# Expert slots of a fused attention and two-MoE kernel: gathers three slots ahead, their transposes two, expert reads behind the slot's last transpose

## The chip, the cores and the metric

The kernel runs on one core of a Trainium2 chip. The metric is the device time of one execution in microseconds (us); less is better. A core has five engines with an instruction queue each: TensorE (PE, with PEld for its weight loads), VectorE (DVE), ScalarE (ACT), GpSimd (POOL) and SyncE (SP). Each queue is taken strictly in order. DMAs are issued from a queue (here SP for plain and transposing ones, POOL for indirect ones) and then moved by 16 DMA engines.

## The reference

Three layers follow each other: an attention with exponential features, a gated feed-forward layer, and a mixture of 8 experts in which each token goes to one expert. The change lies in the third:

```python
logits = x @ w_gate + modality_bias[modality_id]
e_idx = np.argmax(logits, axis=1)
...
for e in range(E):
    mask = e_idx == e
    ...
    h = np.maximum(x[mask] @ w1[e], 0.0)
    out[mask] = gate_w[mask, None] * (h @ w2[e])
```

There are 2304 tokens, model width 512, expert width 1024. For the inputs of the reference the experts get 0, 374, 0, 493, 297, 564, 576 and 0 tokens.

## The kernel before

The third layer works in *slots* of 128 tokens of one expert. Every value is held as two half-precision parts, high and low, and a product is three matmuls. A slot `j` takes these steps:

- `gather(j)` (L927): an indirect DMA from POOL's queue fetches the slot's 128 token rows (`xg`, 256 KB) from `xs` in DRAM, by indices that the routing has worked out (`IDX`).
- `xtr(j)` (L933): a transposing DMA on SP's queue makes `xT` of it.
- `wload(j, part)` (L954): SP reads two numbers from SBUF into registers (L956 the expert, L957 whether it differs from the expert that this set of weight tiles already holds), and issues the expert's weights, 2 MB for each part, in two pieces of 1 MB (L963). The pieces are conditional: where the expert is the same, nothing is moved, but the instruction stays in the queue with its waits. There are two sets of weight tiles, L1_0/L2_0 for even slots and L1_1/L2_1 for odd ones; part 0 (L1) waits until `mm1` of slot j-2 has read the set, part 1 (L2) until `mm2` of slot j-2 has.
- `mm1(j)` (L965): 24 matmuls of 512 columns (L973) into two banks; ACT (L976) and DVE (L977) make the two parts of each half of `hs`, and SP transposes each half into `hsT` (L979).
- `mm2(j)` (L982): 24 matmuls (L989), 12 for each half of `hsT`; DVE scales the result (L992), and POOL scatters it to the output (L993).

Slots 0 to 3 are routed from the first 14 of the 18 tiles of tokens, slots 4 and up from all 18, after a second routing step (`hook`) that runs beside the first slots and ends with 18 small matmuls (`inv`, L759). 20 slots always run; three conditional pieces follow, which these inputs do not take.

`run_slots` (L996) writes the steps in the code's order, but what each engine's queue holds is set by a scheduler: the program is built with `schedule_with_timeline_sim=True`, and a model of the times places each instruction as early as the model thinks it can run. `tc.issue_after(x)` keeps what is written under it behind the instruction x. So the order of the queues, printed below, counts, and not the order of the code. The buffers are three `xg`, three `xT` and four `hsT`.

Of the kernel before, what the change touches and what calls it, by code (L numbers as in the profile page):

```python
# [42 lines left out]
M8 = 20  # L43
# [4 lines left out]
def _weave(main, side, lead=0.0):  # L48

    main, side = list(main), list(side)  # L50
    done = 0
    for i, m in enumerate(main):
        m()
        want = min(len(side), int(math.ceil(len(side) * (i + 1) / (len(main) * (1.0 - lead)))))
        while done < want:
            side[done]()
            done += 1
    for s in side[done:]:
        s()
# [3 lines left out]
def body(ctx, tc, k0, kt0, q0, qt0, kk, kkt, qq, qqt, vv, vvt, w_phi, w_gv, w_out, rms_g, mid, w_g2, mbias,  # L63
         w1, w2, consts, out):
    nc = tc.nc
    V, A, G, SP, PE = nc.vector, nc.scalar, nc.gpsimd, nc.sync, nc.tensor
# [855 lines left out]
    IDX, GT, CTL = {}, {}, {}  # L922


    X, HH = {}, {}

    def gather(j):  # L927
        x = (m2 if j >= 2 else xp).tile([128, 2 * DM], F16, tag="xg2", bufs=3 if j >= 2 else 2, name="xg2")
        G.indirect_dma_start(out=x, out_offset=None, in_=xs[0:128 * TA] if j < KA else xs,
                             in_offset=bass.IndirectOffsetOnAxis(ap=IDX[j][0], axis=0))  # L930
        X[j] = x

    def xtr(j):  # L933
        t = (m2 if j >= 2 else xp).tile([128, 8, 128], F16, tag="xT2", bufs=3 if j >= 2 else 2, name="xT2")
        SP.dma_start_transpose(out=t, in_=X[j])
        X[j] = t

    reg = {}

# [11 lines left out]
    def lane_tile(part, lane):  # L951
        return L1[lane].rearrange("p a h l f -> p (a h l f)") if part == 0 else L2[lane].rearrange("p a l f -> p (a l f)")

    def wload(j, part):  # L954
        if part == 0:
            reg[j] = (SP.value_load(CTL[j][0], min_val=0, max_val=NE - 1),  # L956
                      SP.value_load(CTL[j][1], min_val=0, max_val=1))  # L957
        e, need = reg[j]
        src = (ws1, ws2)[part][bass.ds(e, 1)].rearrange("e p f -> (e p) f")
        dst = lane_tile(part, j % 2)  # L960
        for i in range(2):
            sl = slice(4096 * i, 4096 * i + 4096)
            SP.dma_start(out=dst[:, sl], in_=src[:, sl], cond=need, cond_hint=False)  # L963

    def mm1(j, halves=(0, 1)):  # L965
        x, w = X[j], L1[j % 2]
        HH.setdefault(j, [])
        for half in halves:
            p = ps_gv.tile([128, 512], F32, tag="gv", name="m2h") if half == 0 else ps_pj.tile([128, 512], F32, tag="pj", name="m2h")
            n = 0  # L970
            for kc in range(4):
                for xl, wl in PAIRS:
                    PE.matmul(p, lhsT=x[:, 4 * xl + kc, :], rhs=w[:, kc, half, wl, :], start=(n == 0), stop=(n == 11))  # L973
                    n += 1
            hs = m2.tile([128, 2, 512], F16, tag="hs", bufs=4, name="hs")
            A.activation(out=hs[:, 0], in_=p, func=AF.Relu)  # L976
            V.scalar_tensor_tensor(out=hs[:, 1], in0=p, scalar=0.0, in1=hs[:, 0], op0=ALU.max, op1=ALU.subtract)  # L977
            t = m2.tile([128, 8, 128], F16, tag="hsT", bufs=4, name="hsT")
            SP.dma_start_transpose(out=t, in_=hs.rearrange("p a f -> p (a f)"))  # L979
            HH[j].append(t)  # L980

    def mm2(j):  # L982
# [13 lines left out]
    def run_slots(j0, j1, hook=None, started=False):  # L996
        if not started:
            for j in range(j0, min(j0 + 2, j1)):
                gather(j)
                wload(j, 0)  # L1000
                wload(j, 1)
            xtr(j0)
            mm1(j0)
        for j in range(j0, j1):
            if hook is not None:
                hook(j)
            if j + 2 < j1:
                gather(j + 2)
            if j + 1 < j1:
                xtr(j + 1)  # L1010
                mm1(j + 1)
            if j + 2 < j1:
                wload(j + 2, 0)
            mm2(j)
            if j + 2 < j1:
                wload(j + 2, 1)
# [45 lines left out]
    for b in range(4):  # L1062
# [10 lines left out]
        if b == 0:  # L1073
            w = []
            for i, s in enumerate(m0):
                if i % 2 == 0:
# [18 lines left out]
    m7, m8 = group_steps(7, 6), group_steps(8, 7)  # L1095
# [2 lines left out]
    _weave(m7[M7:] + m8[:M8], mixed(w2s[n:], guess(), ra))  # L1098
    wp_ctx.close()
    xp = ctx.enter_context(tc.tile_pool(name="xp", bufs=2, side="right", reuse_waits="tile"))  # L1100
    _weave(m8[M8:], [lambda: gather(0), lambda: gather(1), lambda: xtr(0), lambda: wload(0, 0), lambda: wload(0, 1),
                     lambda: wload(1, 0), lambda: wload(1, 1)])
    for s in out_steps(8):
        s()
# [8 lines left out]
    def hook(j):  # L1113
        while rb and j >= HOOKJ[len(HOOKJ) - len(rb)]:
            used_i[0] = rb.pop(0)()

    mm1(0, (0,))
    for i in range(2):
        with tc.issue_after(last[i]):
            if i == 0:  # L1120
                mm1(0, (1,))
            else:
                run_slots(0, NSURE, hook, True)
    used = nc.values_load(used_i[0], min_val=0, max_val=NSLOT)  # L1124
    for j0, j1 in ((20, 21), (21, 23), (23, 25)):
        with tc.If(used > j0):
            run_slots(j0, j1)
# [72 lines left out]
```

## Time and profile before

| | us |
|---|---|
| median of 3 runs | 941.72 (937.82 to 948.75) |
| the profiled execution | 947.29 |
| its span, first to last instruction | 945.5 |
| TensorE busy in the span | 831.9 (88%) |
| VectorE busy | 525.8 (56%) |
| SP queue's transfers, share of 16 DMA engines | 76.1% |

The durations below come from the profiled execution, which took 1.8 us more than its span. The slots fill the last 240 us of the span. "SPq" rows are DMA issues on SP: the time from the first issue of a run of like ones to the end of the last, not the transfer. An `L` in a row is a weight tile, `m2h` the result of `mm1`, `m2y` that of `mm2`.

### The profile page before, as it was taken

How to read it: one execution, taken by the hardware profiler on the slowest of the kernel's cores; microseconds unless marked ns; L12 is line 12 of the kernel's file. 1: busy time of each engine (PE TensorE's matmuls, PEld its weight loads, DVE VectorE, ACT ScalarE, POOL GpSimd, SP SyncE). 2: the span in 40 equal slices, each digit the busy share in tenths (PEclk: the TensorE clock that was granted, in tenths of full speed). 3: DMA queues.
4: the chain of work that ended last, by engine and by line, in shares of the span. 5: the costliest groups of instructions: out<-in, count | busy, mean ns of one | idle time of the engine just before them, and what ended most of it. 6: DMA issues, size and time to landing. Idle time of an engine off the chain costs nothing. (4 is left out here: it accounts for less than half of the span.)

```text
span 945.5 us, 18474 instructions
## 1 busy us (share of the span) xinstructions
PE 831.9 (88%) x6760; PEld 569.7 (60%) x6760; DVE 525.8 (56%) x1160; ACT 423.9 (45%) x1093; POOL 383.4 (41%) x384
## 2 busy tenths in 40 slices
PE   8944989978978988788998899998999787999995
PEld 7833778557567657476766578675764333444442
DVE  7788788877556755568767744347726211222221
ACT  5666446556466866776557734334321010111110
POOL 1567645347255945547745535121220212121001
PEclk9755989999999999999999989999999988999998
DMA  8778778599888989898979853997995389799631
GB/s 297 198 189 186 178 168 214 171 227 236 211 209 248 273 253 237 235 238 224 238 216 224 203 115 57 330 333 250 284 320 105 101 214 191 145 287 241 168 87 51
DMA packets 266591, 197.40 MB, mean 209 GB/s; under 512 B 212863, under 2 KB 214271, under 8 KB 262912
## 3 DMA queue, kind: packets, MB, share of 16 engines
q1 hardware_dynamic: 263296, 186.21, 76.1%
q0 software_dynamic: 3200, 9.97, 3.2%
q8 instruction: 55, 0.90, 0.4%
q14 instruction: 40, 0.33, 0.1%
HBM read 164.92 MB, written 43.52 MB: 220 GB/s over the span
## 5 line engine op out<-in xcount | busy, mean ns | idle before, releaser
L515 PE MATMUL gv<-xT,wgv 128*128 128x256 f16 x2304 | 285.7, 281 | 25.4 <-DVE hu L525 18.4
L515 PEld LDWEIGHTS <-wgv 128*128 128x128 f16 x2592 | 254.6, 100 | 70.8 <-issue 26.3
L152 POOL TENSOR_TENSOR hT<-hu,hT 128x256 f16<-128x256 f32 x108 | 84.8, 785 | 197.1 <-ACT hT L151 191.7
L631 DVE SCALAR_TENSOR_TENSOR w2b<-w2a,w2b 128x512 f16<-128x512 f32 x128 | 107.1, 837 | 94.2 <-ACT w2b L630 93.5
L537 PE MATMUL po<-wo,hT 128*128 128x512 f16 x648 | 155.0, 388 | 0.5 <-POOL wo L152 0.3
L630 ACT ACTIVATE w2b<-w2a 128x512 f16<-128x512 f32 x128 | 81.2, 635 | 109.2 <-DMA w2a<-in_w_dram 101.9
L989 PE MATMUL m2y<-L,hsT 128*128 128x512 f16 x480 | 109.8, 385 | 8.2 <-DMA hsT<-hs 8.2
L152 POOL TENSOR_TENSOR eq<-e,eq 128x512 f16<-128x512 f32 x72 | 90.3, 1260 | 63.9 <-DVE eq L149 28.4
L973 PE MATMUL m2h<-L,xT 128*128 128x512 f16 x480 | 109.7, 385 | 5.5 <-DMA xT<-xg 5.3
L976 ACT ACTIVATE hs<-m2h 128x512 f16<-128x512 f32 x40 | 23.9, 597 | 193.4 <-PE m2h L973 181.5
L537 PEld LDWEIGHTS <-hT 128*128 128x128 f16 x648 | 62.8, 100 | 68.7 <-issue 7.6
L989 PEld LDWEIGHTS <-hsT 128*128 128x128 f16 x480 | 47.3, 99 | 66.4 <-DMA hsT<-hs 9.2
L973 PEld LDWEIGHTS <-xT 128*128 128x128 f16 x480 | 47.4, 99 | 64.1 <-DMA xT<-xg 5.8
L977 DVE SCALAR_TENSOR_TENSOR hs<-m2h,hs 128x512 f16<-128x512 f32 x40 | 27.6, 691 | 99.7 <-ACT hs L976 99.1
L523 DVE SCALAR_TENSOR_TENSOR th<-th,gv 128x256 f32<-128x256 f32 x108 | 44.6, 413 | 53.2 <-ACT th L522 52.7
L993 POOL DMA_INDIRECT out_dram<-y,ixB x16 | 16.0, 997 | 127.1 <-DVE y L992 110.6
L151 ACT CAST hT<-hu 128x256 f16<-128x256 f32 x108 | 43.7, 405 | 46.8 <-DVE hu L525 46.4
L360 ACT ACTIVATE e<-pj,b 128x128 f32<-128x128 f32 x144 | 54.0, 375 | 9.7 <-POOL eq L152 8.1
L387 PE MATMUL oo<-kv,eT 128*128 128x65 f16 x768 | 33.7, 204 | 27.0 <-DMA eT<-eq 25.5
L522 ACT ACTIVATE th<-gv 128x256 f32<-128x256 f32 x108 | 41.5, 384 | 34.9 <-PE gv L515 34.6
L361 ACT ACTIVATE e<-pj,b 128x128 f32<-128x128 f32 x144 | 54.7, 380 | 0.2 <-DVE b L354 0.2
L320 PE MATMUL kv<-v,ek 128*128 128x65 f32 (+1 forms) x320 | 49.5, 300 | 2.7 <-ACT ek L296 2.6
(229 smaller groups left out, 1157.7 us busy)
## 6 DMA issues: line engine op xcount, KB each, us to landing
L<-ws SPq DMA_DIRECT2D x88, 1024.0 KB
w2a<-in_w_dram SPq DMA_DIRECT2D x128, 256.0 KB
ws<-w2b SPq DMA_DIRECT2D x128, 256.0 KB
wst<-in_w_gv_dram SPq DMA_DIRECT2D x24, 512.0 KB
wst<-in_w_out_dram SPq DMA_DIRECT2D x12, 512.0 KB
xs<-x SPq DMA_DIRECT2D x18, 256.0 KB
v<-in_vv_dram SPq DMA_DIRECT2D x16, 260.0 KB
k<-in_kk_dram SPq DMA_DIRECT2D x12, 256.0 KB
```

The source lines that it names most:

```text
L151: A.copy(dst_hi, src)
L152: (V if lo == "v" else G).tensor_tensor(out=dst_lo, in0=src, in1=dst_hi, op=ALU.subtract)
L320: PE.matmul(acc[:, s, :], lhsT=l, rhs=r_, start=(n == 0), stop=(n == len(ops) - 1))
L360: A.activation(out=e[:, r, 0, :], in_=pp[:, j, :], func=AF.Exp, scale=sc, bias=b1[:, j:j + 1])
L361: A.activation(out=e[:, r, 1, :], in_=pp[:, j, :], func=AF.Exp, scale=-sc, bias=b2[:, j:j + 1])
L515: PE.matmul(p[:, which, :], lhsT=w[:, kc, wl, f], rhs=x[:, 4 * xl + kc, :], start=(n == 0), stop=(n == 11))
L523: V.scalar_tensor_tensor(out=t, in0=t, scalar=1.0, in1=p[:, 0, :], op0=ALU.add, op1=ALU.mult)
L537: PE.matmul(p, lhsT=hT[g, c][:, hl, tk], rhs=wo[:, c, wl, :], start=(c == 0 and hl == 0 and wl == 0), stop=(c == 11 and hl == 1))
L630: A.activation(out=o[:, :, 0, :], in_=t, func=AF.Copy, scale=WS)
L631: V.scalar_tensor_tensor(out=o[:, :, 1, :], in0=t, scalar=WS, in1=o[:, :, 0, :], op0=ALU.mult, op1=ALU.subtract)
L973: PE.matmul(p, lhsT=x[:, 4 * xl + kc, :], rhs=w[:, kc, half, wl, :], start=(n == 0), stop=(n == 11))
L989: PE.matmul(p, lhsT=t[:, 4 * hl + i, :], rhs=w[:, fc, wl, :], start=(fc == 0 and hl == 0 and wl == 0), stop=(fc == 7 and hl == 1))
```

## The change

The gather of a slot is written three slots ahead in place of two, its transpose two slots ahead in place of one, and `wload` of part 0 (the two register reads and the L1 pieces) of slot j+2 is kept behind the last `hsT` transpose of slot j.

```diff
     def xtr(j):
         t = (m2 if j >= 2 else xp).tile([128, 8, 128], F16, tag="xT2", bufs=3 if j >= 2 else 2, name="xT2")
-        SP.dma_start_transpose(out=t, in_=X[j])
         X[j] = t
+        SP.dma_start_transpose(out=t, in_=G2.pop(j))
...
-            SP.dma_start_transpose(out=t, in_=hs.rearrange("p a f -> p (a f)"))
+            LAST[j] = SP.dma_start_transpose(out=t, in_=hs.rearrange("p a f -> p (a f)")).ins
...
             xtr(j0)
             mm1(j0)
+            if j0 + 1 < j1:
+                xtr(j0 + 1)
+        else:
+            gather(j0 + 2)
         for j in range(j0, j1):
             if hook is not None:
                 hook(j)
+            if j + 3 < j1:
+                gather(j + 3)
             if j + 2 < j1:
-                gather(j + 2)
+                xtr(j + 2)
             if j + 1 < j1:
-                xtr(j + 1)
                 mm1(j + 1)
             if j + 2 < j1:
-                wload(j + 2, 0)
+                with tc.issue_after(LAST.pop(j)):
+                    wload(j + 2, 0)
             mm2(j)
...
-    _weave(m8[M8:], [lambda: gather(0), lambda: gather(1), lambda: xtr(0), lambda: wload(0, 0), lambda: wload(0, 1),
+    _weave(m8[M8:], [lambda: gather(0), lambda: gather(1), lambda: xtr(0), lambda: xtr(1), lambda: wload(0, 0), lambda: wload(0, 1),
```

How the scheduled queues differ, at the three places that matter below. First SP's queue from the `hsT` transposes of slot 3 to the token transpose of slot 4 (`xT_10719` before, `xT_10631` after), before the change:

```order
L979 DMA_TRANSPOSE hsT<-hs 128x8x128 x2
L956 TENSOR_LOAD ctlB
L956 ISA x2
L963 ISA
L963 DMA L_0_8739<-ws_74 128x4096
...
L963 DMA L_1_8738<-ws_73 128x4096
L957 TENSOR_LOAD ctlB
L957 ISA x2
...
L935 DMA_TRANSPOSE xT_10719<-xg_10625 128x8x128
```

The second "..." stands for eight more such reads, L956 and L957 in turn; nine others stand right ahead of the first row. After the change:

```order
L979 DMA_TRANSPOSE hsT<-hs 128x8x128 x2
L963 ISA
L963 DMA L_0_8739<-ws_74 128x4096
L956 TENSOR_LOAD ctlB
L956 ISA x2
L957 TENSOR_LOAD ctlB
L957 ISA x2
L963 ISA
L963 DMA L_0_8739<-ws_74 128x4096
...
L963 DMA L_1_8738<-ws_73 128x4096
L936 DMA_TRANSPOSE xT_10631<-xg_10537 128x8x128
```

Nine reads between became two, and both pieces of slot 4's second weights (`L_0_8739`) stand behind the `hsT` transposes, the two reads between them.

Second, TensorE's queue where `mm1` of slot 5 ends, before the change (`xT_10811` is slot 5, `xT_10903` slot 6):

```order
L973 LDWEIGHTS xT_10811
L973 MATMUL m2h<-L_1_8738,xT_10811 128x512
L973 LDWEIGHTS xT_10903
L973 MATMUL m2h<-L_0_8737,xT_10903 128x512
L973 LDWEIGHTS xT_10903
```

After the change (`xT_10723` is slot 5; `L_0_8739` with `hsT` is `mm2` of slot 4):

```order
L973 LDWEIGHTS xT_10723
L973 MATMUL m2h<-L_1_8738,xT_10723 128x512
L989 LDWEIGHTS hsT
L989 MATMUL m2y<-L_0_8739,hsT 128x512
L989 LDWEIGHTS hsT
```

Before, `mm1` of slot 6 begins right behind `mm1` of slot 5; after, all of `mm2` of slot 4 and half of `mm2` of slot 5 (36 matmuls) stand ahead of it, and `mm1` of slot 7 ahead of `mm2` of slot 6.

Third, SP's queue around the first weights of slot 6 (`L_0_8737`) and the first piece of its second weights (`L_0_8739`), before the change; the four `hsT` rows are the halves of slots 4 and 5, `xT_10995` is slot 7, `xT_11087` slot 8:

```order
L963 DMA L_0_8737<-ws_73 128x4096
L979 DMA_TRANSPOSE hsT<-hs 128x8x128
L963 ISA
L963 DMA L_0_8737<-ws_73 128x4096
L979 DMA_TRANSPOSE hsT<-hs 128x8x128
L935 DMA_TRANSPOSE xT_10995<-xg_10901 128x8x128
L979 DMA_TRANSPOSE hsT<-hs 128x8x128
L935 DMA_TRANSPOSE xT_11087<-xg_10993 128x8x128
L979 DMA_TRANSPOSE hsT<-hs 128x8x128
L963 ISA
L963 DMA L_0_8739<-ws_74 128x4096
```

After the change, where both `hsT` rows are slot 5:

```order
L979 DMA_TRANSPOSE hsT<-hs 128x8x128
L957 TENSOR_LOAD ctlB
L957 ISA x2
L963 ISA
L963 DMA L_0_8737<-ws_73 128x4096
L963 ISA
L963 DMA L_0_8737<-ws_73 128x4096
L979 DMA_TRANSPOSE hsT<-hs 128x8x128
L963 ISA
L963 DMA L_0_8739<-ws_74 128x4096
```

The first weights (`L_0_8737`) moved behind the first `hsT` transpose of slot 5, both pieces together, and the first piece of the second weights (`L_0_8739`) now follows one transpose later in place of five.

## Rows read from the trace of the kernel before

**Rows 1.** TensorE's timeline, slots 2 to 19: start us, us, engine line operation.

```profile
735.40 2.75 PE L989 MATMUL m2y<-L,hsT 128*128 128x512 f16 x12
...
743.17 2.75 PE L989 MATMUL m2y<-L,hsT 128*128 128x512 f16 x12
748.49 5.35 PE L989 MATMUL m2y<-L,hsT 128*128 128x512 f16 x24 [2.56 <-DMA hsT<-hs]
759.15 15.64 PE L973 MATMUL m2h<-L,xT 128*128 128x512 f16 x60 [5.30 <-DMA xT<-xg]
774.63 2.75 PE L989 MATMUL m2y<-L,hsT 128*128 128x512 f16 x12
777.58 1.89 PE L973 MATMUL m2h<-L,xT 128*128 128x512 f16 x8 [0.20 <-DMA L<-ws]
...
782.76 5.34 PE L989 MATMUL m2y<-L,hsT 128*128 128x512 f16 x24
793.72 5.07 PE L989 MATMUL m2y<-L,hsT 128*128 128x512 f16 x12 [5.62 <-DMA hsT<-hs]
798.62 5.34 PE L973 MATMUL m2h<-L,xT 128*128 128x512 f16 x24
...
853.01 5.34 PE L989 MATMUL m2y<-L,hsT 128*128 128x512 f16 x24
...
925.53 10.52 PE L989 MATMUL m2y<-L,hsT 128*128 128x512 f16 x48
```

**Rows 2.** Busy time by stretch: us, PE PEld DVE ACT POOL, granted PE clock, DMA, GB/s.

```profile
759.15:765.00 5.85, 5.85 (x16) 2.20 (x17) 0.00 (x0) 0.53 (x1) 1.95 (x2) 0.56 0.67 148
...
793.70:798.60 4.90, 4.88 (x12) 1.76 (x13) 0.00 (x0) 0.00 (x0) 0.67 (x1) 0.52 0.98 283
798.60:935.70 137.10, 137.10 (x637) 62.15 (x635) 27.73 (x39) 15.52 (x26) 21.20 (x22) 1.00 0.68 169
```

**Rows 3.** SP's timeline of DMA issues, 735 to 797 us.

```profile
735.74 3.58 SPq L963 DMA_DIRECT2D L<-ws  x4
745.23 2.62 SPq L979 DMA_TRANSPOSE hsT<-hs  x2
749.79 0.83 SPq L963 DMA_DIRECT2D L<-ws  x3
755.86 6.73 SPq L935 DMA_TRANSPOSE xT<-xg  x3
...
767.90 0.34 SPq L963 DMA_DIRECT2D L<-ws  x1
...
782.44 0.33 SPq L963 DMA_DIRECT2D L<-ws  x1
782.87 1.30 SPq L979 DMA_TRANSPOSE hsT<-hs  x1
...
789.57 7.09 SPq L979 DMA_TRANSPOSE hsT<-hs  x1
```

**Rows 4.** The tile hs on DVE, 741 to 747 us: min/median/max ns, first and last start.

```profile
L977 DVE SCALAR_TENSOR_TENSOR hs<-m2h,hs x2: 691/692/692, 742.7 to 744.0; 128x512 f16<-128x512 f32 x2
```

**Rows 5.** Register reads on SP by line, 750.5 to 756 us.

```profile
L956 SPq TENSOR_LOAD <-ctlB x4: 262/267/273, 751.3 to 754.7; - x4
...
L957 SPq TENSOR_LOAD <-ctlB x5: 262/270/272, 750.7 to 755.2; - x5
```

**Rows 6.** POOL's timeline, the first gather of the second routing step (slot 4).

```profile
736.55 0.98 POOL L929 DMA_INDIRECT xg<-xs,ixB  x1 [3.75 <-DVE iBg L768]
```

**Rows 7.** DMA queues (packets, MB, share) and issues by line, 700 to 946 us.

```profile
q1 hardware_dynamic: 67520, 29.50, 55.4%
...
L<-ws SPq DMA_DIRECT2D x72, 1024.0 KB
```

**Rows 8.** SP's timeline of DMA issues around slot 11.

```profile
826.45 2.21 SPq L963 DMA_DIRECT2D L<-ws  x4
...
838.47 1.78 SPq L963 DMA_DIRECT2D L<-ws  x4
...
844.24 5.76 SPq L979 DMA_TRANSPOSE hsT<-hs  x2
```

More of the change, by code (lines that the diff above doesn't have):

```diff
@@ L922, in body @@
     IDX, GT, CTL = {}, {}, {}
-    X, HH = {}, {}
+    X, G2, HH, LAST = {}, {}, {}, {}
     def gather(j):
@@ L930, in gather @@
                              in_offset=bass.IndirectOffsetOnAxis(ap=IDX[j][0], axis=0))
-        X[j] = x
+        G2[j] = x
     def xtr(j):
         t = (m2 if j >= 2 else xp).tile([128, 8, 128], F16, tag="xT2", bufs=3 if j >= 2 else 2, name="xT2")
-        SP.dma_start_transpose(out=t, in_=X[j])
         X[j] = t
+        SP.dma_start_transpose(out=t, in_=G2.pop(j))
     reg = {}
```

## The prediction

> **What bounds the kernel now.** I read the clock and the share of TensorE over the span first, then TensorE's timeline over the last stage (the 20 slots of the second mixture of experts), then the DMA issues of SP beside it. In the timeline [rows 1] a slot is two blocks: 24 matmuls of `mm1` (L973) and 24 of `mm2` (L989). From 798.62 to 925.53 us stand 588 matmuls, 126.91 us, so 215.8 ns each, 5.18 us a block and 10.36 us a slot; TensorE is busy for all 137.10 us of that stretch at full clock [rows 2]. There nothing can be gained by ordering. Before it the timeline has holes. After the routing matmuls (from 735.40 us) 840 matmuls are left; at 215.8 ns they take 181.3 us and would end at 916.7 us. They end at 925.53 + 10.52 = 936.05 us, of which 0.16 us is the drawn-out end of the last one. So 19.2 us are lost, all between 745 and 799 us:
>
> - before `mm2` of slot 3: 748.49 - (743.17 + 2.59) = 2.7 us, for the transpose of `hs`
> - before `mm1` of slot 4: 759.15 - (748.49 + 5.18) = 5.5 us, for the transpose of the gathered tokens
> - 60 matmuls from 759.15 to 774.63: 15.48 us where 12.95 are due, 2.5 us
> - before the second half of `mm1` of slot 6: 0.4 us, for its weights
> - before the first half of `mm2` of slot 6: 793.72 - (782.76 + 5.18) = 5.8 us
> - 12 matmuls from there: 4.90 us where 2.59 are due, 2.3 us.
>
> The third and sixth are the clock: 0.56 and 0.52 of full speed, which is the 1.2 GHz level, right behind the two long holes [rows 2]. The hole of 2.7 us left no such mark: the blocks behind it run at 5.18 us.
>
> Who makes the holes? On SP [rows 3] the issues are in one line. After four weight issues end at 735.74 + 3.58 = 739.32 us, the next one, the `hs` transposes of slot 3, starts at 745.23 us, though the first `hs` was ready at 742.7 + 0.7 = 743.4 us [rows 4]. The order on SP has nine register reads in between (of expert numbers for slots far ahead). The same again: the weight issues from 749.79 end at 750.62 us, the transpose of slot 4 starts at 755.86 us, and between them stand nine reads; five of L957 and four of L956 lie in 750.5 to 756 us, 0.26 to 0.27 us of load each [rows 5], and with the register work behind each load 5.24 / 9 = 0.58 us a read. The gather of slot 4 was not to blame: its indices were there at 736.55 us [rows 6].
>
> The hole at slot 6 is another one. Few weight loads really run: 72 pieces of 1 MB are issued from 700 us on, but the SP queue moved 29.5 MB there [rows 7], of which some 61 transposes and two stores take 0.26 MB each, 16.5 MB. That leaves 13 MB, three slots of 4 MB. Counting tokens per expert in the reference's inputs (0, 374, 0, 493, 297, 564, 576, 0) puts them at slots 6, 11 and 14. Slot 6 is the bad one: TensorE takes it right behind slots 4 and 5, so its first weights wait for the late `mm1` of slot 4, its second weights for the late `mm2` of slot 4 (issued from 782.44 us), and the `hs` transposes queue behind them (782.87, then one that holds SP for 7.09 us) [rows 3].
>
> **The change, part by part.** Gathers: three ahead in the code; but the POOL queue has them in the same places as before up to slot 9, so nothing, either way (a gather that came 1 us later would cost 0 where TensorE has 10 us of cover, and at most that 1 us at slot 4). Transposes two ahead: in the full stretch the scheduler already had a slot's token transpose ahead of the `hs` transposes of the slot three earlier, and `mm1` never waits there [rows 2], so nothing there. Issuing a slot's reads and first weights behind the last `hs` transpose: this spreads the reads, two a slot. No read is added; four A-phase reads move from before 690 us to slots 0 and 1. TensorE has no hole there (its first is at slot 3), so I take 0 for it, between a loss and a gain of 0.5 us.
>
> I walk TensorE's new order with 2.59 us a half block and 5.18 us a block. The 120 slot matmuls ahead of the routing matmuls are the same set, so 735.40 us stands. `mm1` of slot 3 to 740.6, `mm2` of 2 to 745.8, `mm2` of 3 to 750.9, `mm1` of 4.
>
> - *`hs` of slot 3.* Before, its second half was ready at 744.0 + 0.7 us [rows 4], 1.5 us after the block ended at 743.17 [rows 1]; now 742.1 us. From issue to first use took 748.49 - 745.23 = 3.3 us, so even that half is there at 745.4; needed are the first half at 745.8 and the second at 748.4. Hole gone: 2.7 gained.
> - *Tokens of slot 4.* SP now has them behind the second half of slot 4's second weights, which must wait for `mm2` of slot 2 (745.8), and two more weight issues; three issues took 0.83 us, so 746.7 us; issue to use took 759.15 - 755.86 = 3.3, so 750.0 against 750.9. Only 0.9 us to spare: I take a hole of 0.3 us, 0 to 2. Gain 5.5 and the 2.5 of clock, less 0.3.
> - *First weights of slot 6.* They now follow the first `hs` transpose of slot 5. `mm1` of 4 to 756.1, of 5 to 761.3, its first half to 758.7; + 1.5 + 1.3 (a transpose on SP) + 0.6 (a read): 762.1 us, the second piece 762.6. Before, that piece was issued at 767.90 and TensorE had it at 777.58, 9.7 us later: now 772.3. Needed: `mm2` of 4 (to 766.4) and half of `mm2` of 5 (to 769.0) now stand in front, then 12 matmuls, 771.6. Hole 0.7 us, 0 to 3.
> - *Second weights and `hs` of slot 6.* `mm1` of 6 ends at 774.9, then half of 5 (777.5) and `mm1` of 7 (782.7). The first `hs` transpose goes out about 776.2. Before, issue to use was 793.72 - 782.87 = 10.9 us, which would give 787.1, a hole of 4.4. At slot 11 the first weights went out by 828.7 (four issues from 826.45), the second from 838.47, the `hs` transposes from 844.24, and `mm2` started at 853.01 without a wait [rows 8, 1]: 24.3 us from first weights to use were enough, 8.8 us from transpose to use too. Slot 6 now has 762.6 to 782.7, 20.1 us. Bounds 0 and 4.4; I take 2, in the middle.
>
> The Trainium skill (DMA: Bandwidth & Descriptors, Queues, rings and completion order) says that each DMA engine takes the descriptors of one issuing queue in ring order. Rows 3 agree: a transpose behind weights was ready 10.9 us after issue, one without 3.3 us. By that rule alone all that is ahead must have moved first, and with all 4 MB ahead of the transpose the hole would be the upper 4.4 us, the gain 13.8. The new order issues the first half of the second weights some 12 us ahead of the transpose, which is why the sum does not go by that.
>
> What waits behind the new waits: the second weights' second half waits for a whole `mm2` on SP, and behind it stand the next slot's first weights and a token transpose; at slot 4 that is the 0.9 us above, and in the full stretch the transposed tokens are for a slot more than 20 us off.
>
> Sum: 19.2 - 0.3 - 0.7 - 2 = 16.2 us. From the profiled execution's 947.29 us: 931.1. The median of the runs shown is 941.72, 5.6 us lower; the holes are a matter of queue order, not of that difference, so I take the same off it: 925.5 us. In the full stretch SP now also reads registers in every slot: 3 transposes of 1.3, four weight issues of up to 2.2 together, 2 reads of 0.6, 7.3 us of 10.36. Hidden; if not, it is the second rival.
>
> **Rivals.**
> 1. *The weights of slot 6 keep their hole.* For: the load's 4 MB has 4 us less than it had at slot 11. Then 3 + 4.4 us of holes, 2.3 of clock behind them, and 2 at slot 4: gain 19.2 - 11.7 = 7.5, 934 us. Against: slots 11 and 14 show no wait at all.
> 2. *SP becomes the bound: slower.* In the slots with loads SP is held by full queues (5.76 us for two transposes at 844.24 [rows 8], 7.09 for one [rows 3]). If reads and held transposes bring its slot over 10.36 us, tokens come late in every slot from 7 to 19. A slot of 12.5 us costs 2.1 x 12 = 25 us against 16 gained: 951 us. Against: a held queue means that engines are moving data, and only three slots load.
> 3. *The change does not do what it says.* The scheduler had the token transposes early already; if the holes belong to the routing (indices at 736.55) they only move. No change, 941.7. Against: 1.2 to 5.2 us of reads stand in the very gaps.
>
> **How the numbers follow.** Forecast 0.70, first rival 0.17, second 0.06, third 0.07. A measurement here tells about 1% (9.4 us) from nothing. The forecast has all but little of its chance over that, and of the first rival about half: faster 0.77. Same: the rest of these two and the third, 0.17. Slower: the second, 0.06. Range: all bounds at their best give 925.5 - 3 - 0.5, so 922, less a microsecond of spread of the runs: 921; at their worst (2, 3, 4.4, clock 2.3, 0.5) 935, and 2 us more for the spread and the edge of the third rival: 937.
>
> **What would show it.** In TensorE's timeline after: no hole at slots 3 and 4, `mm1` of slot 4 near 751; two reads between weight issues on SP in each slot; clock 1.00 from 735 on; a hole of 0 to 4 us before `mm2` of slot 6; the last matmul near 920. Wrong, if TensorE still stands over 5 us before slot 4 or slot 6, or if holes appear past slot 7.

## The result, and the profile after

The changed kernel takes 936.26 us (median of 20 runs, 929.64 to 940.44), the kernel before 944.75 us (20 runs, 936.02 to 948.75). The ratio is 0.9916, with a 95% interval of 0.9894 to 0.9938: 0.84% of 944.75 us are 7.9 us, between 5.9 and 10.0. The time lies in the range of the forecast (921 to 937 us), near its upper end. The gain is just under half of the 16.2 us that it had worked out, and under the 1% that it had called the least that can be told; with 20 runs of each the interval leaves out 1 all the same.

The page of the changed kernel: busy time, and the granted TensorE clock in 40 slices of 23.4 us. The profiled execution took 939.29 us, its span 937.5.

```profile
PE 825.2 (88%) x6760; PEld 568.7 (61%) x6760; DVE 524.6 (56%) x1160; ACT 424.3 (45%) x1093; POOL 380.9 (41%) x384
...
PEclk9755897999999999999899999999999999999998
```

The busy share of TensorE is the one of before, 88%: holes went, and with them 831.9 - 825.2 = 6.7 us of its busy time, most of which had been half clock (2.5 and 2.3 us in the prediction's list). The timeline shows both. TensorE after, in the same form as [rows 1]; slot 0 starts at 711.07 us, the last `mm2` ends at 917.55 + 10.52 = 928.07 us:

```profile
711.07 2.75 PE L973 MATMUL m2h<-L,xT 128*128 128x512 f16 x12
...
739.49 5.34 PE L973 MATMUL m2h<-L,xT 128*128 128x512 f16 x24
744.66 10.52 PE L989 MATMUL m2y<-L,hsT 128*128 128x512 f16 x48
755.43 10.53 PE L973 MATMUL m2h<-L,xT 128*128 128x512 f16 x48 [0.24 <-DMA xT<-xg]
765.80 7.93 PE L989 MATMUL m2y<-L,hsT 128*128 128x512 f16 x36
774.38 2.75 PE L973 MATMUL m2h<-L,xT 128*128 128x512 f16 x12 [0.65 <-DMA L<-ws]
777.93 2.75 PE L973 MATMUL m2h<-L,xT 128*128 128x512 f16 x12 [0.80 <-DMA L<-ws]
782.39 2.76 PE L989 MATMUL m2y<-L,hsT 128*128 128x512 f16 x12 [1.71 <-DMA hsT<-hs]
784.99 5.34 PE L973 MATMUL m2h<-L,xT 128*128 128x512 f16 x24
791.59 5.35 PE L989 MATMUL m2y<-L,hsT 128*128 128x512 f16 x24 [1.25 <-DMA hsT<-hs]
...
853.76 5.34 PE L989 MATMUL m2y<-L,hsT 128*128 128x512 f16 x24
859.35 5.35 PE L973 MATMUL m2h<-L,xT 128*128 128x512 f16 x24 [0.25 <-DMA L<-ws]
865.74 5.35 PE L989 MATMUL m2y<-L,hsT 128*128 128x512 f16 x24 [1.03 <-DMA hsT<-hs]
...
917.55 10.52 PE L989 MATMUL m2y<-L,hsT 128*128 128x512 f16 x48
```

The blocks of slots 2 to 5 now follow each other: the holes of 2.7 and 5.5 us of before are one of 0.4. At slot 6 there are four short holes in place of a short and a long one, and at slot 14 (859.35 and 865.74) there are two that before did not have. Busy time by stretch after, as in [rows 2]:

```profile
774.38:796.78 22.40, 18.64 (x85) 8.06 (x86) 3.52 (x5) 2.39 (x4) 2.98 (x3) 1.00 1.02 240
796.78:859.35 62.57, 62.32 (x289) 28.09 (x288) 13.02 (x19) 7.16 (x12) 11.97 (x12) 1.00 0.81 211
859.35:870.93 11.58, 10.54 (x49) 4.64 (x49) 1.92 (x3) 1.19 (x2) 1.99 (x2) 1.00 1.13 286
```

The clock is 1.00 in every one, where before had 0.56 and 0.52 [rows 2]. And SP's DMA issues after, as in [rows 3]:

```profile
748.85 2.74 SPq L963 DMA_DIRECT2D L<-ws  x4
751.69 4.32 SPq L936 DMA_TRANSPOSE xT<-xg  x3
...
762.50 4.39 SPq L979 DMA_TRANSPOSE hsT<-hs  x2
768.32 1.04 SPq L963 DMA_DIRECT2D L<-ws  x2
769.47 2.84 SPq L979 DMA_TRANSPOSE hsT<-hs  x1
...
778.52 4.35 SPq L963 DMA_DIRECT2D L<-ws  x4
782.98 1.97 SPq L936 DMA_TRANSPOSE xT<-xg  x1
785.05 4.55 SPq L979 DMA_TRANSPOSE hsT<-hs  x2
```

The gap of 5 us between weight issues and the next transpose, in which SP read registers, is gone (748.85 + 2.74 = 751.59, then 751.69). The first weights of slot 6 go out at 768.32 us, and a transpose right behind them at 769.47.

**How the profiles add up.** I call *stage* the time from the first matmul of slot 0 to the end of the last `mm2`, *ahead* what comes before it; about 11 us of tail follow. Ahead of the stage the kernels differ only in where a few reads and one token transpose stand on SP.

| profile | ahead, us | stage, us | ratio to before, 95% |
|---|---|---|---|
| before, three profiles | 707.0, 714.0, 707.4 | 229.0, 226.1, 227.0 | 1 |
| changed, two profiles | 711.1, 711.7 | 217.0, 218.4 | 0.9916 [0.9894, 0.9938] |
| reads_only | 710.3 | 217.7 | 0.9911 [0.9872, 0.9950] |
| ahead_only | 709.4 | 227.6 | 1.0017 [0.9984, 1.0049] |
| reads_early | 707.0 | 220.8 | 0.9962 [0.9934, 0.9990] |
| before_no_loads | 706.3 | 219.2 | 0.9947 [0.9914, 0.9981] |
| after_no_loads | 710.3 | 210.4 | 0.9839 [0.9799, 0.9879] |
| after_half_loads | 706.9 | 213.3 | 0.9861 [0.9803, 0.9918] |
| weights_early | 706.5 | 218.1 | 0.9914 [0.9885, 0.9943] |
| weights_on_act | 712.0 | 259.2 | 1.0262 [1.0161, 1.0364] |
| weights_early_act | 710.1 | 233.8 | 0.9997 [0.9950, 1.0043] |

The profiles of weights_on_act and weights_early_act are of slow runs of these kernels (982.41 and 956.37 us), while the ratios count the fast ones alone (959.18 and 973.40 us, and 935.90 to 945.24), so in these two rows stage and ratio do not belong together.

With no hole and full clock the stage would be 229.0 - 19.2 = 209.8 us. The time ahead scatters by 7.7 us between two kernels with the order of before (706.3 and 714.0), so two single profiles do not give the gain; the stage does better. On the mean it fell from 227.4 to 217.7, by 9.7 us, which lies within the interval of the ratio.

### The profile page after: what moved, and what is told of

It reads as the page before. It is cut to its first block, busy times and chain, and to the rows that moved or that the text cites. A ratio compares the mean times of both kernels' runs of the same rounds, so it can differ in the third digit from the quotient of the medians.

```text
span 937.5 us, 18475 instructions
## 1 busy us (share of the span) xinstructions
PE 825.2 (88%) x6760; PEld 568.7 (61%) x6760; DVE 524.6 (56%) x1160; ACT 424.3 (45%) x1093; POOL 380.9 (41%) x384
## 5 line engine op out<-in xcount | busy, mean ns | idle before, releaser
L515 PE MATMUL gv<-xT,wgv 128*128 128x256 f16 x2304 | 282.7, 279 | 26.5 <-DVE hu L525 19.4
L537 PE MATMUL po<-wo,hT 128*128 128x512 f16 x648 | 151.5, 382 | 1.9 <-DVE x L545 1.9
L989 PE MATMUL m2y<-L,hsT 128*128 128x512 f16 x480 | 106.7, 379 | 4.0 <-DMA hsT<-hs 4.0
L973 PE MATMUL m2h<-L,xT 128*128 128x512 f16 x480 | 107.0, 379 | 1.9 <-DMA L<-ws 1.7
L976 ACT ACTIVATE hs<-m2h 128x512 f16<-128x512 f32 x40 | 23.9, 597 | 181.4 <-PE m2h L973 181.4
L387 PEld LDWEIGHTS <-eT 128*128 128x128 f16 x768 | 30.9, 105 | 40.1 <-DMA eT<-eq 39.0
```

The costliest lines, as they stand in the source:

```text
L387: PE.matmul(acc[:, j, :], lhsT=et[:, hl * 8 + j * 2 + s, :], rhs=kvs[2 * p + j % 2][:, vl, s, :], start=(n == 0), stop=(n == 5))
L515: PE.matmul(p[:, which, :], lhsT=w[:, kc, wl, f], rhs=x[:, 4 * xl + kc, :], start=(n == 0), stop=(n == 11))
L537: PE.matmul(p, lhsT=hT[g, c][:, hl, tk], rhs=wo[:, c, wl, :], start=(c == 0 and hl == 0 and wl == 0), stop=(c == 11 and hl == 1))
L989: PE.matmul(p, lhsT=t[:, 4 * hl + i, :], rhs=w[:, fc, wl, :], start=(fc == 0 and hl == 0 and wl == 0), stop=(fc == 7 and hl == 1))
```

## The experiments

**The two kernels once more.** Unchanged copies. In the first pair of profiles the stage of the changed kernel was 12.0 us shorter, the whole time only 8: 4.06 us more lay ahead of the stage. One theory was that the change costs something there, the other that this scatters.

> The changed kernel once more, for a second profile. Slot stage is the time from the first mm1 matmul of slot 0 to the end of the last mm2 matmul: 229.0 us before, 217.0 us after in the first two profiles; the part ahead of it was 707.0 us before and 711.1 after. Theory A (the 4.1 us ahead of the stage are scatter between executions): stage 216 to 219 us again, part ahead anywhere in 704 to 712. Theory B (the change itself makes the part ahead longer): part ahead 710 to 712 again. Ratio by both 0.990 to 0.994.

> The kernel before once more, for a second profile. The changed kernel's stage came out at 217.0 and 218.4 us, 11 us under the 229.0 us of before, but its time only 8 us under. Theory C (the first profile of before shows a stage longer than is usual for it, and a part ahead of the stage shorter than usual): stage 223 to 227 us, part ahead 708 to 712 us. Theory D (the stage is what it was, and the change lengthens the part ahead): stage 228 to 230 us, part ahead 706 to 708.

> The kernel before, a third profile. The stage was 229.0 and 226.1 us, and 227.6 us in the kernel with gathers and transposes ahead alone, the part ahead of it between 706.3 and 714.0 us in ten profiles whatever the kernel. Expected: stage 226 to 229 us, part ahead 706 to 714 us.

The second runs of the changed kernel gave 0.9913 [0.9881, 0.9944] and 939.63 us against 946.51, the time ahead 711.65 us. Before's second profile had 714.0 us ahead, its third 707.4. The changed kernel's 711.65 us had fitted both theories; before's 714.0 lies above what either had expected of it, and two kernels with the order of the change have 706.9 and 706.5 (after_half_loads, weights_early). So the 4.06 us are scatter; that the change costs a microsecond or two there is not excluded.

**One half of the change at a time.** Only the rule of order on the reads and first weights, put into the kernel before:

```diff
-            SP.dma_start_transpose(out=t, in_=hs.rearrange("p a f -> p (a f)"))
+            LAST[j] = SP.dma_start_transpose(out=t, in_=hs.rearrange("p a f -> p (a f)")).ins
...
-                wload(j + 2, 0)
+                with tc.issue_after(LAST.pop(j)):
+                    wload(j + 2, 0)
```

> The kernel before with one part of the change: the register reads and first weights of slot j+2 behind the last hsT transpose of slot j; gathers and token transposes written as before. The scheduled queues of TensorE and SP come out as in the changed kernel but for a few rows. Theory A (the register reads made the holes): stage 216 to 220 us, ratio 0.989 to 0.994, as the whole change. Rival (the gathers and transposes written ahead bring the gain): stage 227 to 231 us, ratio 0.998 to 1.002.

And the changed kernel without that rule, so only gathers and transposes further ahead:

```diff
-                with tc.issue_after(LAST.pop(j)):
-                    wload(j + 2, 0)
+                wload(j + 2, 0)
```

> The changed kernel without the rule that keeps reads and first weights behind the last hsT transpose: gathers three and transposes two slots ahead alone. SP again has nine reads ahead of the hsT transposes of slot 3 and nine ahead of the token transpose of slot 4, TensorE's order is that of before. Theory A: stage 227 to 231 us with both long holes and half clock behind them, ratio 0.998 to 1.002. Rival: stage 216 to 220 us, ratio 0.989 to 0.994.

The rule alone gives 0.9911 [0.9872, 0.9950], all of the gain. Gathers and transposes alone give 1.0017 [0.9984, 1.0049], nothing. TensorE's timeline of ahead_only has the holes of before, at their places:

```profile
750.41 5.35 PE L989 MATMUL m2y<-L,hsT 128*128 128x512 f16 x24 [2.08 <-DMA hsT<-hs]
761.05 15.29 PE L973 MATMUL m2h<-L,xT 128*128 128x512 f16 x60 [5.28 <-DMA xT<-xg]
...
794.45 5.29 PE L989 MATMUL m2y<-L,hsT 128*128 128x512 f16 x12 [4.88 <-DMA hsT<-hs]
```

In that of reads_only the wait for slot 4's tokens is 0.28 us, and slot 6 keeps a wait:

```profile
754.67 10.53 PE L973 MATMUL m2h<-L,xT 128*128 128x512 f16 x48 [0.28 <-DMA xT<-xg]
...
790.62 5.35 PE L989 MATMUL m2y<-L,hsT 128*128 128x512 f16 x24 [3.01 <-DMA hsT<-hs]
```

So it is not the tokens that had come late by their own gathers or by the place of their transposes; SP came late to them.

**The reads spread, but the weights free.** The rule moves the reads and the first weights, and with them TensorE's order (`mm1` of slot 6 behind `mm2` of slot 4). Here only the reads are bound, one slot earlier than their weights, and the scheduler goes back to before's order on TensorE:

```diff
-    def wload(j, part):
-        if part == 0:
+    def wread(j):
+        if j not in reg:
             reg[j] = (SP.value_load(CTL[j][0], min_val=0, max_val=NE - 1),
                       SP.value_load(CTL[j][1], min_val=0, max_val=1))
+
+    def wload(j, part):
+        wread(j)
...
-                with tc.issue_after(LAST.pop(j)):
-                    wload(j + 2, 0)
+                wload(j + 2, 0)
             mm2(j)
             if j + 2 < j1:
                 wload(j + 2, 1)
+            if j + 3 < j1 and (j + 3 < KA or j >= 1):
+                with tc.issue_after(LAST[j]):
+                    wread(j + 3)
```

> The changed kernel, with the two reads of a slot split from its first weights: the reads stand behind the last hsT transpose of the slot three ahead, the first weights are free again. TensorE's order is that of before (mm1 of slot 6 right behind slot 5, mm2 of slot 6 right behind slot 5), but SP has one or two reads where before had nine. Theory A1 (the reads alone made the long holes, TensorE's order does not matter): no hole over 1 us ahead of slot 4, stage 216 to 221 us, ratio 0.989 to 0.995. Theory A2 (half of the gain is TensorE's order, which gives the load of slot 6 more time): hole ahead of slot 4 gone, but 5 us or more of holes at slot 6, perhaps with half clock behind them; stage 220 to 226 us, ratio 0.994 to 0.998.

It gives 0.9962 [0.9934, 0.9990], so 3.6 us, under half of the gain; by the stage it is 227.4 - 220.8 = 6.6 us of 9.7, two thirds. TensorE's timeline (lines are three further down, L976 is `mm1`, L992 `mm2`):

```profile
752.50 10.53 PE L976 MATMUL m2h<-L,xT 128*128 128x512 f16 x48 [0.51 <-DMA xT<-xg]
...
765.43 2.75 PE L976 MATMUL m2h<-L,xT 128*128 128x512 f16 x12 [2.40 <-DMA L<-ws]
...
785.71 4.06 PE L992 MATMUL m2y<-L,hsT 128*128 128x512 f16 x12 [4.59 <-DMA hsT<-hs]
```

The wait before slot 4 is gone here too, so the spread reads do that by themselves. At slot 6 stand 2.40 and 4.59 us, the second with half clock behind it (a granted clock of 0.66, and 3.90 us to the next block where 2.59 are due): 8.6 us lost, as before had (0.4 + 5.8 + 2.3). So the second theory of the expectation came true. What TensorE's new order and the later place of the first weights are worth together, most of it at slot 6, is about 220.8 - 217.7 = 3.1 us of stage, or 0.9962 - 0.9911 = 0.51%, 4.8 us, by the ratios; one profile does not decide between the two.

**Without the loads.** To part the reads from the weights, the flag that says whether a slot's expert differs was made zero, in the kernel before and in the changed one; all instructions stay in their queues, and the weight loads of slots 4 to 19 (slots 6, 11 and 14 in fact) move nothing:

```diff
-            V.tensor_tensor(out=ctl[:, 1, 0:2], in0=e[:, 0:2], in1=S["eidA"][:, KA - 2:], op=ALU.not_equal)
-            V.tensor_tensor(out=ctl[:, 1, 2:], in0=e[:, 2:], in1=e[:, 0:NB - 2], op=ALU.not_equal)
+            V.tensor_tensor(out=ctl[:, 1, 0:2], in0=e[:, 0:2], in1=e[:, 0:2], op=ALU.not_equal)
+            V.tensor_tensor(out=ctl[:, 1, 2:], in0=e[:, 2:], in1=e[:, 2:], op=ALU.not_equal)
```

> The kernel before with the weight loads of slots 4 to 19 left out: the register that says whether a load is needed is always 0 there, so slots 6, 11 and 14 and those after them use the wrong expert's weights. Reads, waits and issue order stay. Theory (in the kernel before the two long waits ahead of slot 4 come of the reads, the one at slot 6 of its load): holes of 2.7 and 5.5 us and the half clock behind them stay, those at slot 6 go, stage 219 to 222 us. Rival (the loads hold SP or the DMA engines and so make the holes ahead of slot 4 too): stage 209 to 213 us.

> The changed kernel with the weight loads of slots 4 to 19 left out in the same way. Theory (what holes are left in the changed kernel, 6.7 us at slots 5 to 7 and 13 to 14, come of the loads of slots 6 and 14): stage 210 to 212 us. Rival (they come of the reads that now stand in every slot, or of the order of the transposes): stage 215 to 218 us.

The changed kernel's stage falls to 210.4 us, 0.6 above the one without holes. Before's stays at 219.2. Its TensorE timeline, without loads:

```profile
747.29 7.04 PE L989 MATMUL m2y<-L,hsT 128*128 128x512 f16 x24 [2.09 <-DMA hsT<-hs]
757.87 14.81 PE L973 MATMUL m2h<-L,xT 128*128 128x512 f16 x60 [3.53 <-DMA xT<-xg]
...
780.28 7.93 PE L989 MATMUL m2y<-L,hsT 128*128 128x512 f16 x36
```

The holes of slots 3 and 4 are there with no load running, those of slot 6 are not: two troubles, as the prediction had it. Now each part of the gain has its own number, from one profile of each kernel without loads. Reads: 219.2 - 210.4 = 8.8 us of stage, and by the ratios 0.9947 - 0.9839 = 1.08%, 10.2 us. Loads: they cost 227.4 - 219.2 = 8.2 us of stage before and 217.7 - 210.4 = 7.3 after, so 0.9 us were gained; by the ratios they cost 0.53% before and 0.77% after, so nothing was. The intervals are some 3 us wide to either side, and both ways of reading put the loads' part near nothing.

**Half the bytes.** If the holes at slots 6 and 14 are waits for weights to move, they should shrink with the bytes; if they are waits in SP's order, they should stay. Each piece from slot 4 on loads half of its columns, the other half is left out:

```diff
-            sl = slice(4096 * i, 4096 * i + 4096)
+            sl = slice(4096 * i, 4096 * i + (4096 if j < 4 else 2048))
```

> The changed kernel in which each weight piece of slots 4 to 19 moves only the first half of its columns, so slots 6, 11 and 14 load 2 MB in place of 4 and multiply by weights that are partly those of another expert. The stage was 217.0, 218.4 (changed) and 210.4 us (no loads). If the holes that the change left are the time that the bytes take on the DMA engines: half or less of the 7.3 us stays, stage 211 to 214 us. If any load costs that much by its place among the transposes, whatever its size: 216 to 218 us.

The stage is 213.3 us: 210.4 with none, 217.7 with all, so of the loss of 7.3 us by the loads 2.9 are left with half the bytes. The holes at slot 14 are gone, at slot 6 the first weights and the `hs` of slot 5 still wait, on TensorE:

```profile
771.89 3.83 PE L973 MATMUL m2h<-L,xT 128*128 128x512 f16 x17 [0.88 <-DMA L<-ws]
...
777.63 2.76 PE L989 MATMUL m2y<-L,hsT 128*128 128x512 f16 x12 [1.69 <-DMA hsT<-hs]
```

So the loss goes with the bytes in the main, as the first theory had it, but not everywhere: the wait for the `hs` of slot 5 is 1.69 us with half of them and was 1.71 with all. The ratio's interval, 0.9803 to 0.9918, does not part this kernel from the changed one, and its queue on SP came out a little differently (three weight issues, not two, stand ahead of that transpose), so this rests on one profile.

**First weights written a slot earlier.** If the late issue at 768.32 us is what costs at slot 6, first weights that stand earlier on SP should cure it. They stay behind the same transposes, but come ahead of the second weights of the slot before:

```diff
+        if j0 + 2 < j1:
+            with tc.issue_after(LAST.pop(j0)):
+                wload(j0 + 2, 0)
         for j in range(j0, j1):
...
-            if j + 2 < j1:
-                with tc.issue_after(LAST.pop(j)):
-                    wload(j + 2, 0)
+            if j + 3 < j1:
+                with tc.issue_after(LAST.pop(j + 1)):
+                    wload(j + 3, 0)
```

> The changed kernel with reads and first weights of slot j+3 behind the last hsT transpose of slot j+1, in place of slot j+2 behind slot j: on SP the first weights of a slot now come ahead of the second weights of the slot before it, and do not wait for that mm2. If the holes at slots 6 and 14 come of weights issued too late: stage 212 to 215 us, no wait for weights (L), ratio 0.984 to 0.989. If they come of the 4 MB that must move in any case: stage 216 to 219 us, the waits at other places, ratio 0.990 to 0.994.

0.9914 [0.9885, 0.9943], no better than the changed kernel. TensorE still waits for the first weights of slot 6, here 0.99 us for the first piece, and at slot 14 for `hs`, with half clock behind it (24 matmuls in 7.00 us, granted clock 0.76):

```profile
767.92 2.75 PE L973 MATMUL m2h<-L,xT 128*128 128x512 f16 x12 [0.99 <-DMA L<-ws]
...
870.95 7.00 PE L989 MATMUL m2y<-L,hsT 128*128 128x512 f16 x24 [2.21 <-DMA hsT<-hs]
```

This does not settle the question, because the weights won no time against their use. They went out at 762.58 us at the earliest, and TensorE, which has only `mm2` of slot 4 ahead of `mm1` of slot 6 in this kernel, was due there at 767.92 - 1.15 = 766.77, 4.2 us later; in the changed kernel it is 765.80 + 3 x 2.59 - 768.32 = 5.3 us. Whether an earlier issue would close the holes of slot 6 was not tried.

**Weights from another queue.** If the transposes are late because weights stand ahead of them in SP's queue, weights issued from ACT's queue should free them. The reads and loads of slots 2 to 19 go to ACT, in the changed kernel and in weights_early; `LAST[j]` is then the activation that makes `hs`:

```diff
     def wload(j, part):
+        Q = A if 2 <= j < NSURE else SP
...
-            reg[j] = (SP.value_load(CTL[j][0], min_val=0, max_val=NE - 1),
-                      SP.value_load(CTL[j][1], min_val=0, max_val=1))
+            reg[j] = (Q.value_load(CTL[j][0], min_val=0, max_val=NE - 1),
+                      Q.value_load(CTL[j][1], min_val=0, max_val=1))
...
-            SP.dma_start(out=dst[:, sl], in_=src[:, sl], cond=need, cond_hint=False)
+            Q.dma_start(out=dst[:, sl], in_=src[:, sl], cond=need, cond_hint=False)
```

> The changed kernel with reads and weights of slots 2 to 19 issued by ACT, behind its last hs of the slot, in place of SP; SP issues transposes alone. The loads move the same bytes on the same 16 DMA engines, from another queue. Theory E (the transposes of hs wait for the weights ahead of them in SP's queue): holes for hsT at slots 5, 6 and 13 gone or under 1 us in all, stage 211 to 214 us, ratio 0.983 to 0.988. Theory F (the engines are full, whatever the queue): stage 216 to 219 us, ratio 0.990 to 0.994. If ACT, now holding reads and waits, makes hs late: stage over 219 us.

> As the kernel with the weights on ACT, and with reads and first weights of slot j+3 behind the last hs of slot j+1, so that they do not wait for an mm2. Theory E with time to spare for the loads: stage 210.5 to 213 us, ratio 0.981 to 0.987. Theory F: 216 to 219 us.

Neither theory came true: 1.0262 [1.0161, 1.0364], and 0.9997 with the weights a slot earlier. Every run of weights_on_act (959.18 to 992.69 us) is longer than the longest of the kernel before beside it (950.90). TensorE's timeline of weights_on_act, then SP's, around the load of slot 6; the wait is for the `hs` of slot 5:

```profile
796.65 8.02 PE L990 MATMUL m2y<-L,hsT 128*128 128x512 f16 x24 [18.04 <-DMA hsT<-hs]
```

```profile
772.86 19.09 SPq L936 DMA_TRANSPOSE xT<-xg  x1
792.04 2.98 SPq L980 DMA_TRANSPOSE hsT<-hs  x1
```

SP has no weights in its queue, and yet one transpose takes 19.09 us to issue. The expectation had a third case, that ACT makes `hs` late. ACT did, for slot 6, whose first half of `mm1` ended at 772.74 us and whose first `hs` ACT began at 777.36, behind weight issues:

```profile
769.04 8.11 ACTq L964 DMA_DIRECT2D L<-ws  x4
```

But the `hs` of slot 5, for which TensorE waited 18.04 us, ACT had begun at 764.33 and 766.45 us, so ACT did not make that wait. The DMA queues of weights_on_act from 765 to 800 us (packets, MB, share), q1 SP's, q10 ACT's:

```profile
q1 hardware_dynamic: 4019, 1.00, 56.9%
q10 hardware_dynamic: 562, 4.08, 53.9%
```

In the same stretch of the changed kernel SP's queue moved both, transposes and weights:

```profile
q1 hardware_dynamic: 10819, 6.74, 79.1%
```

In 35 us the transposing queue got 1.00 MB through beside 4.08 MB of weights; all in one queue, the same engines moved 6.74 MB. So to take the weights out of SP's queue did not free the transposes: in this profile they came later still. The Trainium skill (DMA: Bandwidth & Descriptors, Rules for kernel authors) says that spreading DMAs over issuing engines does not help bandwidth, since they interleave on the same 16 engines. The runs agree that it does not help; that TensorE waits 18.04 us in one place of this profile is more than the sentence says, and which of the two, the interleaving or the transposes' many small packets (4019 for 1.00 MB), makes it was not tried apart.

No kernel here was clearly faster than the changed one with the computation whole; reads_only and weights_early equal it.

## Why the prediction was right or wrong

Each hole after is the start of a block less the end of the one before, at 2.59 us a half block and 5.18 us a block. Beside what the prediction had for it, in us:

| place | lost before | forecast to stay | stayed |
|---|---|---|---|
| `hs` of slot 3 | 2.7 | 0 | 0 |
| tokens of slot 4 | 5.5 | 0.3 | 0.4 |
| half clock behind it | 2.5 | 0 | 0 |
| first weights of slot 6 | 0.4 | 0.7 | 0.8 + 1.0 |
| `hs` of slot 5, second half | 0 | 0 | 1.9 |
| `hs` of slot 6 | 5.8 | 2 | 1.4 |
| half clock behind it | 2.3 | 0 | 0 |
| slot 14: first weights, then `hs` of slot 13 | 0 | 0 | 0.4 + 1.2 |
| sum | 19.2 | 3.0 | 7.1 |

19.2 - 7.1 = 12.1 us, and the stage of this pair of profiles fell by 229.0 - 217.0 = 12.0: the table is complete for it. Of the 16.2 us forecast, then, 4.1 were lost in the table (7.1 - 3.0), above all at slot 5's `hs` and slot 14, and 2.3 more because before's first profile, from which all was counted, had a stage 1.6 us longer than the mean of three, and the changed kernel's first one 0.7 us shorter than the mean of two. The remaining step from 9.7 to 7.9 us is inside the interval. The time is 936.26 - 925.5 = 10.8 us above the forecast's middle, of which 3.0 are its starting point: 3 runs had given before 941.72 us, 20 gave 944.75. The gain came out under the prediction's own 1%, a case to which it had given 0.17, against 0.77 for more.

**What was right.** The reads: nine of them in one go stood between SP and the transposes of slots 3 and 4, and spreading them gave 8.8 us by the stage without loads (10.2 by the ratios) where 2.7 + 5.5 + 2.5 - 0.3 = 10.4 were forecast. With the loads running and TensorE's order of before (reads_early) it gave 6.6 by the stage and only 3.6 by the ratio, so the size is less sure than the cause. Gathers and transposes further ahead: forecast at nothing, measured at 1.0017. The clock: 1.00 throughout, with no hole over 1.9 us left; that is in part luck, for in other kernels here it fell behind waits of 2.0 us (last section). The full stretch: TensorE is busy for 62.32 of 62.57 us from 796.78, so the second rival, SP as the bound, fell there. The third fell with reads_only.

**The steps that failed are the sizes at the loads**, *First weights of slot 6* and *Second weights and `hs` of slot 6*: 2.7 us left by the forecast, 5.1 by the trace, and 1.6 at slot 14, which had no step at all. With that the prediction's own sign of being wrong, holes past slot 7, came true.

- I let the first weights go out 1.5 + 1.3 + 0.6 = 3.4 us behind half a block of `mm1` of slot 5. That half ends at 755.43 + 3 x 2.59 = 763.2 us, so 766.6 was due; they went out at 768.32. No weights were moving then: from 735 to 768 us SP's queue moved 2.86 MB, which is its 11 transposes of 0.26 MB, and in after_no_loads the same two `hsT` transposes, with the same read between them, take as long:

```profile
761.82 4.55 SPq L979 DMA_TRANSPOSE hsT<-hs  x2
```

  The reads cost more than counted. One stands ahead of the `hsT` transpose of slot 5, which begins at 765.6 us and takes 1.24; the other stands behind it, from 766.9 to 768.0 us. Their loads take 0.69 and 0.80 us (0.84 and 0.80 in after_no_loads), where [rows 5] have 0.26 to 0.27. The first:

```profile
L956 SPq TENSOR_LOAD <-ctlB x1: 688/688/688, 764.6 to 764.6; - x1
```

  I had taken 0.58 us a read from nine in a row, while the DMA engines were idle (busy share 0.00 from 750 to 756 us before, 0.85 from 764 to 768 after), and had counted one of the two; that busy engines are what makes a read slower was not tried by itself. From the end of the issues to its use the second piece then took 777.93 - 769.36 = 8.6 us; the 9.7 taken from before was near.
- I followed the `hs` of slot 6 and forgot that of slot 5. Its second half was issued at 769.47 us, right behind 2 MB of weights, and used at 782.39, 12.9 us later; TensorE could have taken it at 780.52. The forecast put half of that `mm2` block behind `mm1` of slot 6 at no cost. The ring order told of in the prediction may bite here: the rule of the Trainium skill (DMA: Bandwidth & Descriptors, Queues, rings and completion order) was weighed there for the second weights and not for the transpose right behind the first. The trace agrees with it (12.9 us behind weights, 3.3 us with none ahead [rows 1, 3]), but that the ring order is the cause is not shown: in weights_on_act no weights stood ahead on SP, and the transposes were later still.
- `hs` of slot 6 itself cost 1.4 us, in the bounds of 0 and 4.4, but in another way: its transposes were not issued about 776.2 us (780.3 with TensorE's line 4.1 us later in this profile, 739.49 against 735.40) and then slow, they went out at 785.05, behind four weight issues from 778.52 and a token transpose, and TensorE used them 6.5 us later, not 10.9. That 1.4 lies so near the 2 of the forecast is luck.
- At slot 14 I had argued from before that "slots 11 and 14 show no wait at all". That cover was spent: SP's line is longer by two reads in each slot, and everything in it comes later against TensorE. Before, SP around slot 12 (`mm1` of slot 12 ends at 853.01 [rows 1]):

```profile
850.36 1.47 SPq L963 DMA_DIRECT2D L<-ws  x4
...
854.54 2.67 SPq L979 DMA_TRANSPOSE hsT<-hs  x2
857.55 2.19 SPq L963 DMA_DIRECT2D L<-ws  x4
```

After, where `mm1` of slot 12 ends at 843.40 us (853.76 less two blocks of 5.18):

```profile
842.00 3.14 SPq L963 DMA_DIRECT2D L<-ws  x4
...
846.59 2.67 SPq L979 DMA_TRANSPOSE hsT<-hs  x2
849.61 3.48 SPq L963 DMA_DIRECT2D L<-ws  x4
```

A group of four weight issues with its two reads takes 3.14 and 3.48 us in place of 1.47 and 2.19, and the `hs` transposes start 3.2 us behind the block in place of 1.5. The group that holds slot 14's first weights is out by 853.09 us, 5.9 us before TensorE is due there (853.76 + 5.18); before it was out by 859.74, 8.8 us before (the block stood at 853.01 + 3 x 5.18 = 868.55). So the reads were hidden in the slots without loads, as the prediction said, and seem not to be where a load needed those 3 us. Several runs fit this: half the bytes close the holes of slot 14; the three profiles of before and ahead_only, which have the loads without reads in this stretch, show no wait there; and the first weights that were out 7.6 us before their use (slot 11 after: 820.27, then 827.86) or 6.7 (slot 14 in reads_early: 853.08, then 859.78) were not waited for. It is not shown alone, since reads_early has as many reads there and loses only 0.5 us, at the `hs` of slot 14.

**The rivals.** The first, that the weights of slot 6 keep their hole, came nearest in time: a gain of 7.5 us against 7.9. That is partly luck: it left 11.7 of the 19.2 us in the stage, where 7.1 stayed, and only by the scatter of the profiles counted from do 12.1 us become 7.9. It was right in its cause, that the load has too little time, and less so in its size at slot 6 (5.1 us of holes where it had 7.4). The clock stayed full behind these, which are four pieces of under 2 us. Its chance of 0.17 was too low: the argument against it was the slots 11 and 14, and these had more time than slot 6 by the prediction's own count.

## What to carry to other kernels

When a cost is taken out of a queue that also feeds transfers, price what is left there for the loaded case: here a transpose behind 2 MB of loads was used 12.9 us after its issue and one with none ahead 3.3, and a read's load took 0.69 us where 0.27 was counted. Each buffer that is issued near the load (here the one of the slot before) needs its own line in the sum. Reads of registers in bulk ahead of urgent DMAs are worth spreading, but what is spread is paid in each round, and may show where the round has something to hide already. Before an earlier issue is called no cure, see in the trace that it came earlier against its use. Count a gain from several profiles of the stage and not from one pair, when the part ahead of it scatters by as much as the gain.

## What was not expected of the hardware

With two DMA queues the transposes fared worse than with one: 18.04 us of wait and one issue of 19.09 us in the profile of weights_on_act, told of above.

Half clock came behind holes that are no longer than others without it. The third profile of before, on TensorE, and the clock of that stretch:

```profile
748.34 7.04 PE L989 MATMUL m2y<-L,hsT 128*128 128x512 f16 x24 [2.00 <-DMA hsT<-hs]
```

```profile
748.30:755.40 7.10, 7.04 (x24) 2.66 (x24) 0.00 (x0) 0.00 (x0) 0.11 (x1) 0.76 0.21 58
```

And the same block in the first profile of before, behind 2.56 us of wait [rows 1]:

```profile
748.49:753.80 5.31, 5.31 (x24) 2.27 (x24) 0.00 (x0) 0.00 (x0) 0.00 (x0) 1.00 0.26 74
```

24 matmuls took 7.04 us behind a wait of 2.00 us, and 5.31 behind one of 2.56. It was so behind 2.09 us in before_no_loads and 2.21 in weights_early (7.04 and 7.00), and not behind 2.08 in ahead_only (5.35) nor behind 3.01 in reads_only (5.35, granted clock 1.00). So the length of a hole of this size does not say whether the clock falls, and the prediction's "the hole of 2.7 us left no such mark" was one draw. In before's third profile it cost nothing, for the wait for tokens behind it was shorter by as much: `mm1` of slot 4 starts 10.66 us behind the start of this block in both profiles. The half clock behind slot 4's hole is part of the scatter of before's stage, 226.1 to 229.0 us: the 60 matmuls there took 15.48, 14.32 and 14.54 us in the three profiles.

And the scatter ahead of the stage over 14 profiles, 7.7 us from 706.3 to 714.0, both in kernels with the order of before, is as large as the gain of the whole change.
